# A fused attention and MLP block: regrouped heads, single-pass denominators, gate rows behind the first logit slot, and another way of starting

## Chip, cores and metric

The kernel runs on one core of one Trainium2 chip. The metric is the device time of one execution in microseconds (us). PE is the matrix engine, DVE the vector engine, ACT the scalar (activation) engine, POOL the GpSimd engine, SP the engine whose queue issues most of the DMAs. The kernel writes every engine's instructions in a fixed order; semaphores make one engine wait for another.

## What is computed

The input is x of 2048 tokens by 512 features in bf16. The output is `g * a + (1 - g) * b`, where `g = sigmoid(sum(x * gate_w))` is one number per token. The reference, cut to its core:

```
# branch a: 32 heads of 16, 4 segments of 512 tokens
q, k, v = x@wq, x@wk, x@wv              # split into heads and segments
for s in range(4):
    p     = softmax(qs @ ks.T * 0.25 + causal_mask)
    a_dot = p @ vs
    a_mem = (phi(qs) @ M) / (phi(qs) @ z + 1e-6)     # phi(t) = t+1 if t>0 else exp(t)
    o     = gb * a_mem + (1 - gb) * a_dot            # gb = sigmoid(beta), per head
    M, z  = M + phi(ks).T @ vs, z + sum(phi(ks))
a = concat(o) @ wo
# branch b
b = (gelu(x @ w_gate) * (x @ w_up)) @ w_down         # inner width 1792
```

## The kernel before, in words

**Layout.** x is kept transposed in `xT`, features on partitions (4 chunks of 128), tokens along the free axis. q and k of a segment are kept transposed too, in tiles of 128 partitions that hold 8 heads of 16; `c` counts these four groups of heads, `pr = c // 2` the pair they are stored in. A tile of 128 partitions has four strips of 32, `j = 0..3`, each with an even and an odd head; the kernel keeps a second copy of k, `kO`, with the even heads cleared, so that odd heads can be multiplied with strips of 32.

**Phases.** At the start (`first_k`, from L523) PE multiplies a cleared tile six times (L529), then turns the 512 tokens of segment 0 with 16 identity matmuls (L550) into four groups of PSUM banks, and DVE and ACT copy these into `xT` (helper at L314 and L316). Then k of segment 0 is projected (L565), then q and v, and all gate projections of branch b for all segments (L475, evacuated by ACT with GELU at L647). Ahead of the last segment's gate projections stand the gate rows (`gate_rows`, L601): `x * gate_w` summed, 16 column-tiled matmuls with weights that DVE makes in four copies (L662); DVE transposes them (L610), POOL spreads them with 32 small copies over partitions (L618, L619), and behind the first logits ACT takes two exps (L624, L625) and DVE finishes `omz` (L628, L629). `G2` (the exp) is read by all attention results, `omz` by the output.

Then comes attention: 4 segments of 20 logit slots. A slot is 512 columns of row-tiled logits for 4 strips (L735) into two pairs of PSUM banks, two exps on ACT (L757) and two causal selects on POOL (L766). After every five slots two groups `pv` (L785) multiply the probabilities with v, four heads side by side in four column strips; DVE transposes the result (L803), divides, adds the memory part and writes it over `xT` (L829). PE fills the time between slots with column-tiled matmuls, all recorded at L479 by the helper `dense`: up projections (evacuated and multiplied with the GELU on DVE, L657), q, k and v of the next segment, the memory's denominators (`zbd`) and numerators (`Mbd`), and the down and output projections.

**Order.** A planner (`Sched`) writes the order of every engine before the kernel is built: tasks carry costs, priorities, dependencies and rings of buffers, and it gives each PSUM group its banks out of eight. What is written outside it (memsets, masks, loads, in L392 to L438) stands ahead of all its tasks on each engine. `NUPS` says how many of the 56 up groups go into each segment, `SEED` shuffles priorities.

**What the change touches.** `RINGS` (L322), the setup at L384 to L438 with `bd`, a mask of 8 blocks that POOL makes with two selects (L433, L435), after the memset of `vz[0]` (L428) and `hot8` (L429, L430); `first_k`; `gate_rows` and its task `later`; `lhs_rhs` (L709), the dependencies in `logit_slot` (L737), the heads of `pv_group` (L783), `phi` (L842), `m_update` with `zbd` (L921), `mem_den` (L933) and `mem_num` (L965, whose product at L981 is on DVE), and the beta and wo loads (L405, L407).

Today's denominators for a segment are 4 groups of 4 column-tiled matmuls that accumulate into one bank:

```
for c in range(NCH):
    dense(t, zbd[:, c * P:(c + 1) * P], PQ[(s, c // 2)][:, c % 2, :], c == 0, c == NCH - 1)
```

Of the kernel before, what the change touches and what calls it, by code (L numbers as in the profile page):

```python
# [11 lines left out]
BF = dt.bfloat16  # L12
# [24 lines left out]
NWARM = 6  # L37
NUPS = (28, 10, 9, 9)
ATT = 5
SEED = 1  # L40
# [248 lines left out]
def kernel(  # L289
# [22 lines left out]
    def copy(e, dst, src):  # L312
        if e == "ACT":
            nc.scalar.activation(dst, src, AF.Copy)  # L314
        else:
# [6 lines left out]
    RINGS = {"qT": 3, "kT": 3, "kO": 3, "pT": 12, "E": 1, "Q1": 1, "pq": 3,  # L322
             "pkT": 1, "pk": 2, "T": 2, "r": 2, "N": 2, "rm": 1, "Tm": 1, "Nm": 3,
             "osb": 3, "tt": 1}
# [34 lines left out]
    beta8 = ctile("beta8", [8, NCH])  # L359
    bd = ctile("bd", [P, 8, DH])  # L360
    hot8 = ctile("hot8", [8, 8, DH])
# [3 lines left out]
    zbd = ctile("zbd", [P, NCH * (P + 2)])  # L365
# [5 lines left out]
    omg = ctile("omg", [P, NCH], F32)  # L371
    ebr = ctile("ebr", [P, NCH], F32)
    tb = ctile("tb", [P, NCH], F32)
# [13 lines left out]
    gwB = p1.tile([P, FC, 32], BF, name="gwB", tag="gwB")  # L387
# [3 lines left out]
    xn, ident, warm = wdn[:, 0:KT, :], wdn[:, KT, 0:P], wdn[:, KT + 1, :]  # L391
    nc.vector.memset(warm, 0.0)  # L392
# [12 lines left out]
    nc.sync.dma_start(beta8[:, :], A_beta.rearrange("(c h) -> h c", h=8))  # L405
    load_w(nc.sync, wup, B_w_up)
    load_w(nc.sync, wo, A_wo)  # L407

    def ext(at):
        return add("EXT", 0, lambda e: None, lat=at)  # L410

    a_xn = [ext(2700), ext(3200)]
    a_x = [None, ext(18000), ext(22000), ext(26000)]
    a_wk, a_wq = [ext(3900), ext(4200), ext(4500), ext(4800)], ext(5500)
# [12 lines left out]
    nc.vector.memset(zbd[:, :], 0.0)  # L427
# [8 lines left out]
                            compare_op=ALU.is_ge, fill=0.0, base=DH - 1, channel_multiplier=-1)  # L436
    nc.gpsimd.memset(vz[1][:, :, :], 1.0)
# [85 lines left out]
    def first_k():  # L523

        tl = {}

        def f_warm(_):
            for i in range(NWARM):
                nc.tensor.matmul(pair(w)[:, 0, :], lhsT=warm[:, 0:P], rhs=warm,  # L529
                                 start=True, stop=True)  # L530
        w = add("PE", 427 * NWARM, f_warm, prio=-2000, alloc=["pair"])
# [3 lines left out]
        def f_open(_):  # L535
            for i in range(2):
                for h in range(2):
                    tl["x", h, i] = pair(op, h)[:, i, :].rearrange("p (f m) -> p f m", f=2)
                tl["k", i] = pair(op, 2 + i)
                QK[("k", 0, i)] = rtile("kT", [P, 2, L])  # L540
# [4 lines left out]
        for h in range(2):  # L545
            for i in range(2):
                def f_t(_, h=h, i=i):
                    for f in range(2):
                        for m in range(2):
                            nc.tensor.matmul(tl["x", h, i][:, f, m * P:(m + 1) * P],  # L550
                                             lhsT=xn[:, 2 * h + m, (2 * i + f) * P:(2 * i + f + 1) * P],
                                             rhs=ident, start=True, stop=True)
                prev = add("PE", 430, f_t, prio=-1999, deps=[prev, a_xn[h]])
                dst = xT[:, 2 * i:2 * i + 2, h * L // 2:(h + 1) * L // 2]
                xe[h, i] = add("ACT" if i else "DVE", 600,
                               lambda e, dst=dst, k=(h, i): copy(e, dst, tl[("x",) + k][:, :, :]),
                               prio=0, deps=[prev], frees=[(("pair", h), op)])
        a_x[0] = xe[1, 1]
# [3 lines left out]
        for fc in range(FC):  # L562
            def fn(_, fc=fc):
                for c in range(NCH):
# [4 lines left out]
                       deps=[last, xe[0, fc // 2], xe[1, fc // 2], a_wk[fc]])  # L569
# [26 lines left out]
    def gate_rows(prio):  # L596
# [11 lines left out]
        def f_tt(e, t):  # L608
            tl["tt"] = rtile("tt", [P, QB, 32], F32, p1)
            nc.vector.transpose(tl["tt"][:, :, :].rearrange("p a b -> p (a b)"), t[:, :])  # L610

        def f_sp(e):
            z = tl["tt"]
            for s in range(NSEG):
                src = slice(32 * s, 32 * s + 32)
                for j in range(4):
# [4 lines left out]
                        z[src, :, :].rearrange("p (kt a) b -> p a kt b", a=4)[:, j, :, 0])  # L621

# [9 lines left out]
        tt = evac("DVE", g, box, f_tt, alloc=["tt"])  # L632
        TAB["zsp"] = add("POOL", 4000, f_sp, deps=[tt], prio=6, frees=[("tt", tt)])

        def later():
            TAB["g2"] = add("ACT", 500, f_ex, deps=[TAB["zsp"], TAB["first_x"]], prio=2)
            TAB["omz"] = add("DVE", 250, f_om, deps=[TAB["g2"]], prio=5)
        TAB["later"] = later
# [26 lines left out]
    def f_bps(t):  # L665
        nc.tensor.matmul(t[:, 0:NCH], lhsT=hot8[:, :, :].rearrange("p a b -> p (a b)"),  # L666
                         rhs=beta8[:, :], start=True, stop=True)
# [5 lines left out]
    def f_eb(e):  # L673
        nc.vector.reciprocal(ebr[:, :], omg[:, :])
# [4 lines left out]
    def f_wo(e):  # L679
        for c in range(NCH):  # L680
            nc.vector.tensor_scalar_mul(wo[:, c, :], wo[:, c, :], omg[:, c:c + 1])
# [6 lines left out]
    for s in range(NSEG):  # L688
        if s == 3:
            gate_rows(-960 + 20 * s)  # L690
        for hp in range(HS // 2):
            gate_pair(s, hp, -959 + 20 * s + hp)
            if s == 1 and hp == HS // 2 - 1:
                g, box = group("bps", 60, f_bps, -922, [a_be])
                t_tb = evac("ACT", g, box, lambda e, t: nc.scalar.activation(
                    tb[:, :], t[:, 0:NCH], AF.Tanh, scale=0.5), cost=250)
# [7 lines left out]
    opened = add("EXT", 0, reopen, deps=list(GM.values()) + [TAB["zsp"]])  # L704
# [3 lines left out]

    def lhs_rhs(s, c, e, j, kt, qb, nq):  # L709
        pr, i = c // 2, c % 2  # L710
# [5 lines left out]
    def logit_slot(s, t):  # L716
# [20 lines left out]
        deps = [EVQK[("q", s, c)]]  # L737
        if w <= 2:
            deps.append(EVQK[("k", s, c)])
        if w >= 2:  # L740
            deps.append(EVQK[("o", s, c)])
# [5 lines left out]
        if w == 4 and c % 2 == 1:  # L747
            pr = c // 2
            frees = [(n + "T" if n != "o" else "kO", first_ev[(n, s, pr)]) for n in "qko"]
            if s == 0:  # L750
# [354 lines left out]
```

## Time and profile before

| what | value |
|---|---|
| median of 3 runs | 274.99 us (274.38 to 275.15) |
| the profiled execution | 274.56 us, of which the span of its instructions is 272.7 us |
| busy in the span: PE, ACT, DVE, POOL | 266.6, 211.6, 171.5, 106.2 us |
| start of k's projection (L565) | 6.05 us |
| gate rows (L601) start | 52.97 us |
| first logit slot (L735) | 66.14 us |
| last slot of the last segment | 255.96 us |
| denominators (L479 on zbd) | 48 matmuls, 3.1 us busy |
| Nm product on DVE (L981) | 12 times 855 ns |

All starts are counted from the span's start. A row of a timeline gives start, length, engine, line, operation, the tiles it writes and reads, how many instructions were merged, and in brackets how long its engine was idle before and who ended that. Matmuls overlap in the array, so that one matmul's recorded length is longer than the distance between the starts of two.

### The profile page before, as it was taken

How to read it: one execution, taken by the hardware profiler on the slowest of the kernel's cores; microseconds unless marked ns; L12 is line 12 of the kernel's file. 1: busy time of each engine (PE TensorE's matmuls, PEld its weight loads, DVE VectorE, ACT ScalarE, POOL GpSimd, SP SyncE). 2: the span in 40 equal slices, each digit the busy share in tenths (PEclk: the TensorE clock that was granted, in tenths of full speed). 3: DMA queues.
4: the chain of work that ended last, by engine and by line, in shares of the span. 5: the costliest groups of instructions: out<-in, count | busy, mean ns of one | idle time of the engine just before them, and what ended most of it. 6: DMA issues, size and time to landing. Idle time of an engine off the chain costs nothing.

```text
span 272.7 us, 10273 instructions
## 1 busy us (share of the span) xinstructions
PE 266.6 (98%) x4569; PEld 127.0 (47%) x4575; DVE 171.5 (63%) x323; ACT 211.6 (78%) x234; POOL 106.2 (39%) x209
## 2 busy tenths in 40 slices
PE   7999999999999999999999999999999999999995
PEld 4444444444444554454444454444444444444454
DVE  3340003000888898989998989999858698765140
ACT  3445555646987799998978998899998999889812
POOL 8100000070343444355444545455555456664500
PEclk9999999999999999999999999999999999999999
DMA  7994790000023000220001121000000000000002
GB/s 210 369 135 97 256 352 10 0 0 2 5 45 38 2 2 2 41 43 2 2 23 22 42 41 41 5 2 2 22 22 4 22 24 2 22 22 22 22 5 78
DMA packets 22244, 14.02 MB, mean 51 GB/s; under 512 B 14136, under 2 KB 21176, under 8 KB 22200
## 3 DMA queue, kind: packets, MB, share of 16 engines
q1 hardware_dynamic: 21624, 12.85, 17.9%
q8 instruction: 35, 0.57, 0.9%
q10 hardware_dynamic: 576, 0.52, 0.6%
q14 instruction: 9, 0.07, 0.1%
HBM read 8.13 MB, written 2.10 MB: 37 GB/s over the span
## 4 chain that ended last, share of the span: by engine, by line
PE 97%; ACT 1%; issue 1%; DVE 0%; ACTq 0%
PE ps L479 57%; PE ps L475 20%; PE ps L735 10%; PE ps L785 6%; PE ps L565 1%; PE ps L529 1%; ACT pT L757 1%; PE ps L894 1%; PE ps L550 0%; PE ps L601 0%; DVE xT L316 0%; ACT osb L1017 0%; DVE wdn L392 0%; PE ps L666 0%; ACTq L1017 0%
## 5 line engine op out<-in xcount | busy, mean ns | idle before, releaser
L757 ACT ACTIVATE pT<-ps 128x1024 bf16<-128x1024 f32 x160 | 153.7, 1031 | 15.9 <-PE ps L735 14.7
L766 POOL TENSOR_SCALAR_AFFINE_SELECT pT<-pT 128x512 bf16<-128x512 bf16 (+1 forms) x160 | 94.3, 592 | 104.0 <-ACT pT L757 103.2
L479 PE MATMUL ps<-wdn,G 128*32 128x512 bf16 (+1 forms) x952 | 59.1, 368 | 0.2 <-ACT pT L757 0.2
L479 PE MATMUL ps<-xT,wup 128*32 128x512 bf16 x896 | 55.5, 380 | 0.0
L657 DVE TENSOR_TENSOR G<-ps,G 128x512 bf16<-128x512 f32 x56 | 37.8, 680 | 18.3 <-PE ps L479 18.0
L475 PE MATMUL ps<-xT,wga 128*128 128x512 bf16 x219 | 48.4, 379 | 0.4 <-issue 0.2
L647 ACT ACTIVATE G<-ps 128x1024 bf16<-128x1024 f32 x28 | 28.7, 1024 | 23.5 <-PE ps L475 22.8
L475 PEld LDWEIGHTS <-wga 128*128 128x128 bf16 x224 | 21.7, 98 | 26.4 <-issue 0.4
L803 DVE STREAM_TRANSPOSE T<-ps 128x512 f32<-128x512 f32 x32 | 22.7, 708 | 17.7 <-PE ps L785 11.6
L479 PEld LDWEIGHTS <-wup 128*32 128x32 bf16 x896 | 23.2, 96 | 21.1 <-issue 2.1
L479 PEld LDWEIGHTS <-G 128*32 128x32 bf16 x952 | 22.4, 96 | 19.4 <-issue 4.2
L618 POOL COPY G_87<-tt 32x16 f32<-32x16 f32 x16 | 3.1, 195 | 47.8 <-DVE tt L610 47.2
L735 PE MATMUL ps<-qT,kT 16*128 16x256 bf16 (+2 forms) x320 | 17.4, 274 | 0.0
L735 PE MATMUL ps<-qT,kO 32*128 32x128 bf16 (+2 forms) x320 | 17.3, 272 | 0.0
L479 PE MATMUL ps<-wo,xT 128*32 128x512 bf16 (+1 forms) x272 | 16.5, 367 | 0.0
L479 PEld LDWEIGHTS <-xT 128*32 128x32 bf16 x464 | 11.5, 96 | 10.3 <-issue 2.1
L735 PEld LDWEIGHTS <-kT 16*128 16x128 bf16 x320 | 6.8, 92 | 18.9 <-issue 18.8
L735 PEld LDWEIGHTS <-kO 32*128 32x128 bf16 x320 | 6.9, 92 | 12.1 <-issue 12.0
L479 PE MATMUL ps<-xT,wq 128*32 128x512 bf16 x192 | 12.5, 380 | 0.0
L479 PE MATMUL ps<-xT,wk 128*32 128x512 bf16 x192 | 12.5, 380 | 0.0
L1017 ACT ACTIVATE osb<-ps,omz 128x512 bf16<-128x512 f32 (+1 forms) x8 | 5.1, 635 | 9.4 <-PE ps L479 9.4
L479 PE MATMUL ps<-wv,xT 128*32 128x512 bf16 x192 | 12.4, 381 | 0.0
(116 smaller groups left out, 249.6 us busy)
## 6 DMA issues: line engine op xcount, KB each, us to landing
out_dram<-osb SPq DMA_DIRECT2D x15, 128.0 KB, 1.8
wup<-in_B_w_up_dram SPq DMA_DIRECT2D x1, 1792.0 KB, 8.2
wdn<-in_B_w_down_dram SPq DMA_DIRECT2D x1, 1792.0 KB, 13.7
wga<-in_B_w_gate_dram SPq DMA_DIRECT2D x1, 1280.0 KB, 10.2
wq<-in_A_wq_dram SPq DMA_DIRECT2D x1, 512.0 KB, 4.8
wga<-in_B_w_gate_dram SPq DMA_DIRECT2D x1, 512.0 KB
wv<-in_A_wv_dram SPq DMA_DIRECT2D x1, 512.0 KB, 7.3
wo<-in_A_wo_dram SPq DMA_DIRECT2D x1, 512.0 KB, 9.3
```

What stands on the lines that cost most here:

```text
L475: nc.tensor.matmul(t, lhsT=lhsT, rhs=rhs, start=start, stop=stop)
L479: nc.tensor.matmul(t[a, :], lhsT=lhsT[:, a], rhs=rhs, start=start, stop=stop, tile_position=(0, 32 * j), skip_group_check=True)
L529: nc.tensor.matmul(pair(w)[:, 0, :], lhsT=warm[:, 0:P], rhs=warm, start=True, stop=True)
L618: nc.gpsimd.tensor_copy(G2[dst, s, :], z[src, :, 0])
L647: ge = evac("ACT", g, box, lambda e, t: nc.scalar.activation(dst, t[:, :, :], AF.Gelu_apprx_tanh), cost=920, ring="pair")
L657: UPT[(s, hs)] = evac("DVE", g, box, lambda e, t: nc.vector.tensor_mul(G[:, s, hs, :], t[:, :], G[:, s, hs, :]))
L735: nc.tensor.matmul(A[j // 2][:, j % 2, at * P:(at + nq) * P], lhsT=l, rhs=r, start=True, stop=True, tile_position=(32 * j, 0))
L757: nc.scalar.activation(pT[(s, t, h)][:, :, :], A[h][:, :, :], AF.Exp, scale=0.25)
L766: nc.gpsimd.affine_select(out=v, in_=v, pattern=pat, compare_op=ALU.is_ge, fill=0.0, base=0, channel_multiplier=-1)
L785: nc.tensor.matmul(t[32 * j:32 * j + 32, qb * P:(qb + nq) * P], lhsT=vz[s % 2][:, kt, h * VW:h * VW + 32], rhs=pT[(s, t0 + w, j // 2)][:, ...
L803: nc.vector.transpose(TT[key][:, e, :, :].rearrange("p a b -> p (a b)"), t[:, :])
L1017: nc.scalar.activation(bx["o"][:, cols], bank(first)[:, cols], AF.Copy, scale=f)
```

## The change

The same work is grouped otherwise. Strip j of a logit slot takes its head from group (c + j) % 4 instead of c, so that the four column strips of a `pv` result hold heads of all four groups; strip q holds group q. `mem_num` follows, and `mem_den` becomes one pass of four column-tiled matmuls, each with another moving operand; its weights come from `zmask`, which 16 small copies on DVE make out of `bd` during setup. The rows of `wo` are loaded in the new order with 16 loads instead of one, and a second set of beta in the new order with 16 more. All q, k and kO of a segment are due at its first slot, with rings of 4 instead of 3. The gate rows move behind slot 0; their transposed tile uses the ring `Tm`, and the POOL copies become four tasks. The Nm product moves from DVE to POOL; `phi` writes in place. PE warms up with eleven matmuls of 256 columns on the constant 1.0 instead of six of 512 on a cleared tile; x of segment 0 is turned token tile by token tile, evacuated by DVE (0, 2), ACT (1) and both (3). `NUPS` and `SEED` change.

```diff
-NWARM = 6
-NUPS = (28, 10, 9, 9)
+NWARM = 11
+NUPS = (27, 9, 9, 11)
...
-SEED = 1
+SEED = 3
...
-    RINGS = {"qT": 3, "kT": 3, "kO": 3, "pT": 12, "E": 1, "Q1": 1, "pq": 3,
+    RINGS = {"qT": 4, "kT": 4, "kO": 4, "pT": 12, "E": 1, "pq": 2,
              "pkT": 1, "pk": 2, "T": 2, "r": 2, "N": 2, "rm": 1, "Tm": 1, "Nm": 3,
-             "osb": 3, "tt": 1}
+             "osb": 3}
...
+    zmask = ctile("zmask", [P, NCH, 8])
...
+    bsrc = A_beta.rearrange("(q j e) -> j e q", j=4, e=2)
+    nc.sync.dma_start(beta8[0:8, 0, :], A_beta.rearrange("(c h) -> h c", h=8))
+    for q in range(4):
+        for g in range(NCH):
+            nc.sync.dma_start(beta8[2 * q:2 * q + 2, 1, g:g + 1], bsrc[(q - g) % 4, :, q:q + 1])
     load_w(nc.sync, wup, B_w_up)
-    load_w(nc.sync, wo, A_wo)
+    for q in range(4):
+        for g in range(NCH):
+            r0 = P * q + 32 * ((q - g) % 4)
+            nc.sync.dma_start(wo[32 * q:32 * q + 32, g, :], A_wo[r0:r0 + 32, :])
...
-    nc.vector.memset(zbd[:, :], 0.0)
+    nc.vector.memset(zbd[:, :, :], 0.0)
+    nc.vector.memset(zmask[:, :, :], 0.0)
...
                             compare_op=ALU.is_ge, fill=0.0, base=DH - 1, channel_multiplier=-1)
+    for q in range(4):
+        for g in range(NCH):
+            j = (q - g) % 4
+            a = slice(32 * j, 32 * j + 32)
+            nc.vector.tensor_copy(zmask[a, q, 2 * g:2 * g + 2], bd[a, 2 * j:2 * j + 2, 0])
...
+        one = nc.const_aps.tensor(1.0, (P, 256), BF)
+
         def f_warm(_):
             for i in range(NWARM):
-                nc.tensor.matmul(pair(w)[:, 0, :], lhsT=warm[:, 0:P], rhs=warm,
+                nc.tensor.matmul(pair(w)[:, 0, 0:256], lhsT=one[:, 0:P], rhs=one,
                                  start=True, stop=True)
-        w = add("PE", 427 * NWARM, f_warm, prio=-2000, alloc=["pair"])
+        w = add("PE", 214 * NWARM, f_warm, prio=-2000, alloc=["pair"])
...
+        for kt in range(KT):
+            def f_t(_, kt=kt):
+                for f in range(FC):
+                    nc.tensor.matmul(tl["x", kt][:, f, :], lhsT=xn[:, kt, f * P:(f + 1) * P],
+                                     rhs=ident, start=True, stop=True)
+            prev = add("PE", 430, f_t, prio=-1999, deps=[prev, a_xn[kt]])
+            for i, e in ((0, "DVE"), (1, "ACT")):
+                if kt < 3 and i != kt % 2:
+                    continue
+                fs = slice(0, FC) if kt < 3 else slice(2 * i, 2 * i + 2)
+
+                def f_x(e, kt=kt, fs=fs):
+                    copy(e, xT[:, fs, kt * P:(kt + 1) * P], tl["x", kt][:, fs, :])
+                xe[kt, i] = add(e, 600 if kt < 3 else 350, f_x, prio=0, deps=[prev],
+                                frees=[(("pair", kt // 2), op)])
+        a_x[0] = add("EXT", 0, lambda _: None, deps=list(xe.values()))
...
-                       deps=[last, xe[0, fc // 2], xe[1, fc // 2], a_wk[fc]])
+                       deps=[last, xe[2, 0], xe[1, 1], xe[3, fc // 2], a_wk[fc]])
...
-        tt = evac("DVE", g, box, f_tt, alloc=["tt"])
-        TAB["zsp"] = add("POOL", 4000, f_sp, deps=[tt], prio=6, frees=[("tt", tt)])
-
-        def later():
-            TAB["g2"] = add("ACT", 500, f_ex, deps=[TAB["zsp"], TAB["first_x"]], prio=2)
-            TAB["omz"] = add("DVE", 250, f_om, deps=[TAB["g2"]], prio=5)
-        TAB["later"] = later
+        tt = evac("DVE", g, box, f_tt, deps=[opened], alloc=["Tm"])
+        sp = [add("POOL", 1000, f_sp(s), deps=[tt], prio=6, frees=[("Tm", tt)])
+              for s in range(NSEG)]
+        TAB["g2"] = add("ACT", 500, f_ex, deps=sp + [TAB["first_x"]], prio=2)
+        TAB["omz"] = add("DVE", 250, f_om, deps=[TAB["g2"]], prio=5)
...
-        pr, i = c // 2, c % 2
+        pr, i = divmod((c + j) % 4, 2)
...
-        deps = [EVQK[("q", s, c)]]
-        if w <= 2:
-            deps.append(EVQK[("k", s, c)])
-        if w >= 2:
-            deps.append(EVQK[("o", s, c)])
+        deps = [EVQK[(n, s, q)] for n in "qko" for q in range(NCH)] if t == 0 else []
...
-                for j in range(4):
-                    h = 8 * c + 2 * j + e
-                    nc.tensor.matmul(t[32 * j:32 * j + 32, qb * P:(qb + nq) * P],
+                for q in range(4):
+                    j = (q - c) % 4
+                    h = 8 * q + 2 * j + e
+                    nc.tensor.matmul(t[32 * q:32 * q + 32, qb * P:(qb + nq) * P],
                                      lhsT=vz[s % 2][:, kt, h * VW:h * VW + 32],
                                      rhs=pT[(s, t0 + w, j // 2)][:, j % 2, at * P:(at + nq) * P],
                                      start=(kt == 0), stop=(kt == KT - 1),
-                                     tile_position=(0, 32 * j), skip_group_check=True)
+                                     tile_position=(0, 32 * q), skip_group_check=True)
...
+            nc.vector.tensor_mul(zbd[:, :, 0:8], zmask[:, :, :],
+                                 Macc[:, :, 0, DH:DH + 1].to_broadcast((P, NCH, 8)))
...
-            for c in range(NCH):
-                dense(t, zbd[:, c * P:(c + 1) * P], PQ[(s, c // 2)][:, c % 2, :], c == 0,
-                      c == NCH - 1)
-        g, box = group("den", 4 * MM, mms, prio,
+            for q in range(4):
+                nc.tensor.matmul(t[32 * q:32 * q + 32, :], lhsT=zbd[:, q, :],
+                                 rhs=PQ[(s, q // 2)][:, q % 2, :], start=True, stop=True,
+                                 tile_position=(0, 32 * q), skip_group_check=True)
+        g, box = group("den", MM, mms, prio,
...
-            dense(t, Mbd[:, c, :, :].rearrange("p h d -> p (h d)"), PQ[(s, c // 2)][:, c % 2, :],
-                  True, True)
+            for q in range(4):
+                j = (q - c) % 4
+                nc.tensor.matmul(t[32 * q:32 * q + 32, :],
+                                 lhsT=Mbd[:, q, 2 * j:2 * j + 2, :].rearrange("p h d -> p (h d)"),
+                                 rhs=PQ[(s, q // 2)][:, q % 2, :], start=True, stop=True,
...
-            nc.vector.tensor_mul(NMt[(s, c)][:, :, :, :], bx["T"][:, :, :, :],
+            nc.gpsimd.tensor_mul(NMt[(s, c)][:, :, :, :], bx["T"][:, :, :, :],
...
-                        qk_group(s + 1, c, which, n1 + 5 * c - 8, AE)
+                        qk_group(s + 1, c, which, n1 - 10 + 1.5 * c, AE)
...
-                TAB["later"]()
+                gate_rows(-5)
```

## The prediction

> **What bounds the kernel now.** I read the page's engine shares first, then the chain that ended last, then the busy times over the four attention segments, then the timeline of the places that the change touches.
>
> ```profile
> PE 266.6 (98%) x4569; PEld 127.0 (47%) x4575; DVE 171.5 (63%) x323; ACT 211.6 (78%) x234; POOL 106.2 (39%) x209
> ...
> PE 97%; ACT 1%; issue 1%; DVE 0%; ACTq 0%
> ```
>
> PE is busy 98% of the span and is 97% of the chain, so what is added to or taken from PE's stream of work goes into the time at full price, and so does any hole made in it. The other engines cost nothing until PE waits for them.
>
> ```profile
> core 0: us, PE busy (x) PEld busy (x) DVE busy (x) ACT busy (x) POOL busy (x), PEclk, DMA share, GB/s
> 66.14:120.72 54.58, 54.58 (x1151) 26.29 (x1151) 46.03 (x86) 48.55 (x55) 22.29 (x39) 1.00 0.12 20
> 120.72:171.21 50.49, 50.49 (x1069) 23.90 (x1066) 45.89 (x85) 45.34 (x52) 24.62 (x42) 1.00 0.11 26
> 171.21:214.64 43.43, 43.43 (x901) 20.16 (x898) 36.80 (x68) 40.15 (x44) 22.83 (x40) 1.00 0.04 12
> 214.64:255.96 41.32, 40.58 (x824) 18.77 (x821) 28.33 (x48) 37.49 (x41) 22.85 (x39) 1.00 0.06 19
> ```
>
> Each row is one segment, from its first logit slot to the next segment's (the last to its own last slot). PE fills all four, but ACT is at 86 to 92% and DVE at 68 to 91%: a late instruction on either reaches PE soon. Laying out the fillers between slots at 0.216 us per four column tiles of 512 gives 151.9 us; 79 slots take 0.44 us each beside them (a slot with 2.59 of fillers lasted 3.04), together 186.6 of the 189.8 measured. So about 3.2 us is M updates and stalls, and no better order can give back more.
>
> **The start, part by part.** These rows are the first 10 us.
>
> ```profile
> 1.26 2.74 PE L529 MATMUL ps<-wdn 128*128 128x512 bf16 x6 [1.26 <-DVE wdn L392]
> ...
> 3.79 1.69 PE L550 MATMUL ps<-wdn 128*128 128x128 bf16 x16
> 4.47 1.53 DVE L316 CAST xT<-ps 128x512 bf16<-128x512 f32 x2 [2.05 <-PE ps L550]
> 5.02 0.34 POOL L435 TENSOR_SCALAR_AFFINE_SELECT bd<-bd 128x128 bf16<-128x128 bf16 x1
> 6.00 3.16 PEld L565 LDWEIGHTS <-wk 128*128 128x128 bf16 x16 [0.69 <-DMA wk<-in_A_wk_dram]
> 6.05 3.61 PE L565 MATMUL ps<-xT,wk 128*128 128x512 bf16 x16 [0.56 <-DVE xT L316]
> ...
> 29.05 0.44 DVE L662 COPY gwB<-gw 128x32 bf16<-128x32 bf16 x4 [11.75 <-DMA gw<-in_gate_w_dram]
> ```
>
> The first k projection (L565) starts at 6.05, when the evacuations of x are done; its weight load waited for wk until 6.00. So the warm-up on a constant and the finer turning cannot start it before about 6.0: their price is 0, and at most 0.05 is to be had, because wk's landing covers them.
>
> What stands in the way is new. The diff builds zmask with 16 DVE copies of 32x2 out of bd, and in the built order they stand ahead of all evacuations of x on DVE, the first one waiting for POOL's last select on bd. POOL's list up to there is unchanged, so bd is done at 5.02 + 0.34 = 5.36. DVE takes its instructions in order: x waits behind it, though its transposes are ready by about 5.2. No row shows a 32x2 copy. Below, 16 copies at nothing; above, 16 x 0.178, the full duration of one gwB copy, 2.85. I take the distance between the starts of the four gwB copies, (0.44 - 0.178)/3 = 0.087, as the nearest row: 16 x 0.087 = 1.39. Then come three evacuations on DVE (token tiles 0 and 2, half of tile 3): k evacuations, two in 1.29 at 0.69 each, follow each other at 0.60, so 0.60 + 0.60 + 0.42 (between a 128x68 copy at 0.22 and 0.69), and 0.05 to PE. 5.39 + 1.39 + 1.62 + 0.05 = 8.45: PE starts **2.4 later** (1.0 to 3.9 by the bounds). From there to 66.14 PE has no hole above 0.2, so nothing swallows it. Setting bd's selects ahead of vz's memset would take most of it away.
>
> [...]
>
> In that time PE has nothing to do from about 5.2 to 8.45, 3.2 us. The rows show two speeds: the warm-up's six matmuls of 512 start 0.427 apart (2.74 less one duration of 0.63, over 5), L565's sixteen 0.215 apart; the granted clock reads 1.00 in both. PE had worked 3.9 us when the transposes grew faster, near 5.15. If it falls back to the slow pace, some 3.9 us are done at half speed again: up to 2.0 lost. Below, nothing: PE stood idle 0.56 before L565 and stayed fast. I take 0 and keep 2.0 as a case.
>
> [...]
>
> **Denominators.** Today each segment's den takes 16 column-tiled matmuls per group of four c, 48 in all (L479 on zbd, 3.1 us busy, starting 0.054 apart); now 4 per segment. 36 fewer x 0.054 = **-1.94** on PE. That four tiles with four different moving operands still run side by side is shown by L785: 20 matmuls in 0.55 to 0.66, where a quarter of their columns alone is 0.53. The rotation of heads over (c + j) % 4 changes no count and no shape of logits, PV or num.
>
> **Gate rows.** Today they stand between gate projections.
>
> ```profile
> 52.44 0.59 PE L475 MATMUL ps<-xT,wga 128*128 128x512 bf16 x2
> 52.97 1.05 PE L601 MATMUL ps<-xT,gwB 128*32 128x512 bf16 x16
> 54.17 0.59 PE L475 MATMUL ps<-xT,wga 128*128 128x512 bf16 x2 [0.16 <-issue]
> ```
>
> ```profile
> 54.95 0.19 POOL L618 COPY G_87<-tt 32x16 f32<-32x16 f32 x1 [47.22 <-DVE tt L610]
> 55.09 0.18 POOL L619 COPY omz<-tt 32x4 f32<-32x4 f32 x1
> 55.31 0.19 POOL L618 COPY G_87<-tt 32x16 f32<-32x16 f32 x1
> ```
>
> From the last L475 before (52.66) to the next (54.17) pass 1.51; 0.216 belongs to that L475, so the sixteen cost 1.30. Among column-tiled fillers they cost 0.87: **-0.43**. But their POOL copies, 32 in pairs of 0.365 (5.8 us), lost their cover. They ran under gate work; now, behind slot 0 (66.14 in this trace's time), they stand ahead of what the slots need. The sixteen end about 67.5, the DVE transpose (1.19 after their start, 0.72 long) at 68.4, 16 copies at 71.4, two selects of slot 0 (0.41 each) at 72.2, 16 copies at 75.1. On ACT the two exps of the gate (0.25 together) stand ahead of slot 2's exps and wait for that: slot 2's first exp runs 75.4 to 76.4 instead of from about 73.8. In the built order slot 3's logits write the bank that this exp frees. PE, through with slot 2 (73.4) and two up groups, would be there at 75.5: it waits 0.95. Behind it, the next k group needs a bank that DVE frees; on DVE the two omz operations wait for ACT's exps (75.5) ahead of a pkT minimum and that product, which ends at 77.35: another 0.55. A third wait, 0.2, is the second up group's, for the transpose's bank. Sum 1.7, less 0.2 lost in this stretch today (slot 0 lasted 4.01 for 3.45 + 0.44): **+1.5**. Below 0, if exps and fillers close up; above 3, if the copies stretch to one and a half times beside a busy DVE, which no row shows.
>
> **The rest, at nothing.** The Nm product goes from DVE (12 x 0.855 = 10.3) to POOL. POOL's price isn't shown; between its 128x512 select at 0.71 and the 2240-element memset at 1.97, I take 1.0. POOL is at 41 to 55% in the segments and covers it; its queue holds selects behind Nm, and PV waits for those: a late rm could cost some tenths per segment. DVE's relief can give back a part of the 3.2 us of losses. All projections of a segment are now due at its slot 0, with a ring of 4 for that. SP gets 16 small beta loads and 15 more for wo: at 0.45 to 0.5 an issue wup goes out 7 us later, at 34.5, wo and wdn by 43; wup is first read at 66.5, and wo's scaling, 43.25 today, has until the last gate projection. Beta is read near 41 plus the delay and lands near 38. Fillers of the four segments change from 44.8, 41.3, 33.8, 32.0 (before the last slot) to 45.2, 38.9, 34.5, 32.2, and 13.1 behind the last slot stay: PE's balance is kept. I take 0 for all this, within 1.0 either way.
>
> **Sum.** +2.4 - 1.94 - 0.43 + 1.5 = **+1.5** on the profiled execution, 274.56 (span 272.7 and 1.86 around it): 276.1. The median of the runs shown, 274.99, lies 0.43 above it, so **276.5**.
>
> **Rivals.**
> - *PE falls to half pace behind the hole at the start.* For: the hole of 3.2 us, and 3.9 us of work needed at first. Against: the 0.56 of idle that did nothing. +2.0: 278.5.
> - *The gate chain is hidden.* If POOL's copies end by 73.5, ACT never waits, and 1.5 goes: 275.0, no change. For: the planner has 8 banks, and PE has up groups to do. Against: 5.8 us of copies, and slot 3 on the bank of slot 2's exp.
> - *Faster: the fuller DVE queue is what makes today's losses.* DVE loses 10.3 us in segments 1 to 3, 0.909 busy in segment 1. If that takes 1.5 to 2 of the 3.2 us, and the gate chain costs less than 0.5, den and gate rows outweigh the start: 274.99 + 2.4 - 2.4 - 1.8 = 273.2. It decides from 0.8 net gained. Against: PE was busy 50.49 of that segment's 50.49.
> - *The constant warm-up and token tiles start k sooner, as written.* Only if x isn't behind zmask on DVE; wk's landing at 6.00 caps it.
>
> **How the numbers follow.** About 0.3%, 0.8 us, is what a measurement can tell from no change. The worked case has 0.42 (275.4 to 277.6 by its own terms), half pace 0.23, the hidden chain 0.20, faster 0.15. All of the first two end slower, the third within 0.3%. The range takes the first three and their bounds: 274.2 to 278.8.
>
> **What would show it.** Right: DVE's first x evacuation starts near 6.8, behind 16 copies; L584 starts near 8.4; den has 12 matmuls; ACT waits for POOL near 1.5 us ahead of its two short exps. Wrong: copies far from 0.087, L584 below 7.5, L584's sixteen at 0.43 apart (half pace), no ACT wait for POOL, or segments 1 to 3 shorter by more than the den's 0.65 each and their fillers.

## The result, and the profile after

The changed kernel takes 284.0 us (median of 4 runs, 282.27 to 284.73), where the kernel before took 274.94 (274.38 to 275.15) beside it: 1.032 times as long, 95% interval 1.027 to 1.037. The forecast was 276.5, and its range ended at 278.8. The profiled execution of the changed kernel is the longest of its four, 284.73; its span is 283.0, 10.3 longer than that of before.

From the page of the changed kernel, the shares of PE and the other engines, PE's granted clock over 40 slices (the part of the full clock that PE was given, in tenths), and the chain's shares by engine:

```profile
PE 268.6 (95%) x4539; PEld 127.9 (45%) x4544; DVE 169.9 (60%) x328; ACT 212.0 (75%) x235; POOL 116.3 (41%) x221
...
PEclk9579999999997999999999999999999999999999
...
PE 85%; DVE 6%; POOL 4%; ACT 3%; issue 1%; POOLq 0%; ACTq 0%; DVEq 0%
```

PE is still the engine with the most work, but it stands idle for 14.4 us of the span, where it was 6.1: 8.3 of the 10.3 are holes in PE's stream, and its busy time is 2.0 longer. Of the chain 15% now lies elsewhere, where it was 3%: 6% DVE, 4% POOL, 3% ACT. The clock row shows something that before had nowhere: a fall in slices 2 and 3 and another in slice 13. The four segments of the changed kernel, from first slot to first slot:

```profile
core 0: us, PE busy (x) PEld busy (x) DVE busy (x) ACT busy (x) POOL busy (x), PEclk, DMA share, GB/s
73.36:132.47 59.11, 56.55 (x1157) 27.53 (x1158) 48.77 (x92) 48.76 (x55) 29.27 (x72) 0.97 0.10 21
132.47:180.90 48.43, 48.34 (x1024) 22.78 (x1021) 40.64 (x73) 44.40 (x50) 28.31 (x46) 1.00 0.09 22
180.90:224.86 43.96, 43.96 (x913) 20.55 (x911) 35.62 (x65) 41.02 (x46) 24.38 (x43) 1.00 0.06 18
224.86:266.34 41.48, 40.94 (x829) 18.60 (x826) 26.84 (x46) 38.04 (x41) 25.94 (x43) 1.00 0.05 16
```

The first slot comes 7.22 later (73.36 for 66.14). The first segment is 4.53 longer, the second 2.06 shorter, the last two 0.53 and 0.16 longer, the tail 0.09 shorter: together the 10.3. The fillers laid between the slots changed by +0.43, -2.37, +0.65 and +0.21, so the last three segments only follow their share of work. What is lost is lost in two places, ahead of the first slot and in the first segment.

**Ahead of the first slot.** The timeline of the changed kernel around the start (start, length, engine, line, tiles, count, idle time before and who ended it):

```profile
5.04 0.34 POOL L445 TENSOR_SCALAR_AFFINE_SELECT bd<-bd 128x128 bf16<-128x128 bf16 x1
...
5.32 1.96 POOL L452 MEMSET vz_83<- 128x2240 bf16 x1
...
5.41 4.68 DVE L451 COPY zmask<-bd 32x2 bf16<-32x2 bf16 x16 [3.18 <-POOL bd L445]
...
7.22 0.52 POOL L453 MEMSET Mbd<- 128x512 bf16 x1
...
10.01 1.60 DVE L316 CAST xT<-ps 128x512 bf16<-128x512 f32 x3
...
11.67 2.72 PE L584 MATMUL ps<-xT,wk 128*128 128x512 bf16 x6 [6.90 <-DVE xT L316]
```

The shape of the delay is the predicted one: bd, 16 copies, three evacuations, then k. Its size is not: the copies take 4.68, PE stands idle for 6.90, and k starts at 11.67 instead of 6.05. The durations of the 16 copies (shortest, median, longest, in ns):

```profile
L451 DVE COPY zmask<-bd x16: 154/161/2353, 5.4 to 9.9; 32x2 bf16<-32x2 bf16 x16
```

One of them, the first, took 2353 ns; it ended at 7.77, just behind POOL's two memsets (the second ends at 7.74), in whose time it lay. The others last 0.16 each. Then the clock. The busy times of the changed kernel in five stretches (the number before the DMA share is the granted clock):

```profile
7.30:11.60 4.30, 0.00 (x0) 0.00 (x0) 4.14 (x19) 0.00 (x0) 0.45 (x1) 0.50 1.04 370
11.67:17.40 5.73, 5.73 (x14) 2.02 (x14) 0.00 (x0) 0.00 (x0) 0.00 (x0) 0.50 1.03 253
17.60:23.30 5.70, 5.65 (x27) 2.60 (x27) 3.03 (x7) 4.40 (x7) 0.00 (x0) 1.00 0.50 107
82.36:85.77 3.41, 1.47 (x28) 0.75 (x24) 2.70 (x5) 3.35 (x6) 3.00 (x6) 1.00 0.07 15
85.77:89.18 3.41, 3.41 (x49) 1.83 (x42) 1.79 (x4) 1.61 (x2) 0.81 (x2) 0.50 0.41 72
```

PE's hole begins at 4.77; the clock falls 2.5 later, and the half clock holds from 7.26 to 17.50. In it 14 matmuls of k start in 5.73, 0.427 apart; from 17.5 they are 0.216 apart. The 5.62 of a later start, 2.9 of half pace, less the 1.30 of gate rows that moved away, make the 7.22.

**In the first segment.** The gate rows behind slot 0, same kernel:

```profile
75.56 0.19 POOL L637 COPY G_89<-Tm 32x16 f32<-32x16 f32 x1 [67.81 <-DVE Tm L629]
...
82.42 0.26 ACT L644 ACTIVATE G_89<-G_89 128x64 f32<-128x64 f32 x1 [1.92 <-POOL G_89 L637]
...
82.81 0.44 DVE L648 TENSOR_SCALAR omz<-omz 128x16 f32<-128x16 f32 x1 [1.08 <-ACT omz L645]
...
83.74 0.40 PE L753 MATMUL ps<-qT,kO 32*128 32x512 bf16 x4 [1.07 <-ACT pT L770]
...
85.01 1.21 PE L494 MATMUL ps<-xT,wk 128*32 128x512 bf16 x16 [0.87 <-DVE G L675]
```

This is the predicted chain: POOL's copies until 82.5, ACT's short exps behind them (1.92 of idle), slot 3's logits behind the exp that frees their bank (1.07), the next k group behind DVE (0.87). Slots 0 to 3 lasted 4.04, 3.04, 3.31 and 6.2, where their fillers and the usual 0.44 make 4.0, 3.04, 2.17 and 3.57. The waits account for 2.1 (1.14 in slot 2, 0.95 in slot 3, by the traces of kernels below in which the clock stayed up and slot 3 lasted 4.52). The other 1.7 is the second fall of the clock, 85.77 to 89.18, behind a stretch in which PE was idle for 1.94 of 3.41.

### The profile page after: what moved, and what is told of

It reads as the page before. It is cut to its first block, busy times and chain, and to the rows that moved or that the text cites. A ratio compares the mean times of both kernels' runs of the same rounds, so it can differ in the third digit from the quotient of the medians.

```text
span 283.0 us, 10243 instructions
## 1 busy us (share of the span) xinstructions
PE 268.6 (95%) x4539; PEld 127.9 (45%) x4544; DVE 169.9 (60%) x328; ACT 212.0 (75%) x235; POOL 116.3 (41%) x221
## 4 chain that ended last, share of the span: by engine, by line
PE 85%; DVE 6%; POOL 4%; ACT 3%; issue 1%; POOLq 0%; ACTq 0%; DVEq 0%
PE ps L494 47%; PE ps L490 19%; PE ps L753 8%; PE ps L799 6%; ACT pT L770 2%; PE ps L584 2%; DVE zmask L451 2%; POOL G_89 L637 1%; POOL omz L638 1%; PE ps L978 1%; POOL vz_82 L438 1%; PE ps L906 1%; DVE xT L316 1%; DVE T L817 0%; DVE G L675 0%
## 5 line engine op out<-in xcount | busy, mean ns | idle before, releaser
L779 POOL TENSOR_SCALAR_AFFINE_SELECT pT<-pT 128x512 bf16<-128x512 bf16 (+1 forms) x160 | 91.6, 577 | 82.5 <-ACT pT L770 81.7
L494 PE MATMUL ps<-wdn,G 128*32 128x512 bf16 (+1 forms) x952 | 59.8, 368 | 0.0
L637 POOL COPY G_89<-Tm 32x16 f32<-32x16 f32 x16 | 3.4, 213 | 68.4 <-DVE Tm L629 67.8
L494 PEld LDWEIGHTS <-xT 128*32 128x32 bf16 x464 | 12.1, 96 | 9.8 <-issue 0.6
L629 DVE STREAM_TRANSPOSE Tm<-ps 128x512 f32<-128x512 f32 x1 | 0.7, 716 | 22.0 <-PE ps L620 22.0
L994 POOL TENSOR_TENSOR Nm<-Tm,rm 128x512 bf16<-128x512 f32 x12 | 13.3, 1109 | 1.2 <-DVE N L840 0.9
L314 ACT ACTIVATE kT<-ps 128x512 bf16<-128x512 f32 x7 | 4.0, 601 | 12.7 <-PE ps L584 12.2
L494 PE MATMUL ps<-xT,wq 128*32 128x512 bf16 x192 | 13.5, 401 | 0.0
```

The costliest lines, as they stand in the source:

```text
L494: nc.tensor.matmul(t[a, :], lhsT=lhsT[:, a], rhs=rhs, start=start, stop=stop, tile_position=(0, 32 * j), skip_group_check=True)
L637: nc.gpsimd.tensor_copy(G2[dst, s, :], z[src, :, 0])
L779: nc.gpsimd.affine_select(out=v, in_=v, pattern=pat, compare_op=ALU.is_ge, fill=0.0, base=0, channel_multiplier=-1)
L994: nc.gpsimd.tensor_mul(NMt[(s, c)][:, :, :, :], bx["T"][:, :, :, :], RMt[s][:, :, 2 * c:2 * c + 2][:, :, :, None] .to_broadcast((P, QB, 2, ...
```

## The experiments

The theory after reading the two traces, in two parts. **M:** the mask copies, held by POOL's memset and standing ahead of x on DVE, open PE's hole, and the hole brings the half clock; together some 9 us. **G:** the gate chain on POOL, ACT and DVE costs 2 to 4 in the first segment. The rivals: **S**, that the new warm-up and the turning by token tile make the late start; and, against G, that the first segment is longer through its new order.

**The mask copies out of the way.** They become a task of DVE's, behind gwB's copies near 30 us; all else stays.

```diff
-    for q in range(4):
-        for g in range(NCH):
-            ...
-            nc.vector.tensor_copy(zmask[a, q, 2 * g:2 * g + 2], bd[a, 2 * j:2 * j + 2, 0])
+    add("DVE", 2400, f_zm, deps=[a_gw], prio=4)
```

> The 16 zmask copies are issued later on DVE, behind the gwB copies near 30 us, where DVE is idle; nothing else moves. Theory M (the mask copies ahead of x's evacuations make the loss at the start): the first k projection starts near 6.0 instead of 11.67, its sixteen matmuls stand 0.216 apart, and the time falls by 5.6 + 2.9 = 8.5, from 284.0 to about 275.5. Theory S (turning x by token tile, or warming up on a constant, makes the loss): the time stays within 1 of 284.

275.31 us (274.44 to 278.6, 10 runs), 1.003 times before (0.9997 to 1.006). Its start:

```profile
5.33 1.97 POOL L447 MEMSET vz<- 128x2240 bf16 x1
...
5.91 0.42 DVE L316 CAST xT<-ps 128x256 bf16<-128x256 f32 x1 [0.38 <-ACT xT L314]
...
6.39 2.96 PE L579 MATMUL ps<-xT,wk 128*128 128x512 bf16 x13 [0.93 <-DVE xT L316]
```

POOL's memset is where it was, and the last evacuation of x runs beside it at 0.42: it isn't held. k starts at 6.39 and at full pace. 8.7 of the 9.1 us are gone, by the medians: the copies ahead of x make the loss at the start, hole and half clock together. The same profile, of a run of 276.94, still shows the gate chain (ACT idle 1.95 before its short exp; slots of 4.04, 3.04, 3.35 and 6.12, the last one at half clock from 76.79 on).

**The old start with the copies in place.** Warm-up on a cleared tile with six matmuls, turning by halves, as before the change.

```diff
-NWARM = 11
+NWARM = 6
...
+                    for f in range(2):
+                        for m in range(2):
```

> Warm-up on the cleared tile, turning and evacuation of x as before the change; the mask copies stay where the change put them. Theory M: DVE still reaches x only near 10.0, needs two evacuations instead of three, and k starts near 11.4 at half pace: 283 to 284. Theory S: k starts near 6.05 again and the time is about 275.5.

282.93 us (281.34 to 284.47, 4 runs), 1.031 (1.025 to 1.036):

```profile
10.02 1.27 DVE L316 CAST xT<-ps 128x512 bf16<-128x512 f32 x2
11.34 5.04 PE L581 MATMUL ps<-xT,wk 128*128 128x512 bf16 x16 [6.38 <-DVE xT L316]
```

The evacuations still start at 10.02, k at 11.34. S is rejected: the way PE warms up and x is turned moves k by 0.33, one evacuation less, and not by 5.6.

**POOL's memsets out of the way.** vz[1] and Mbd are cleared by DVE behind gwB, the copies stay ahead of x.

```diff
-    nc.gpsimd.memset(vz[1][:, :, :], 1.0)
-    nc.gpsimd.memset(Mbd[:, :, :, :], 0.0)
+    add("DVE", 2500, f_ms, deps=[a_gw], prio=4)
```

> The memsets of vz[1] and Mbd leave POOL and are issued on DVE behind gwB near 30 us; the mask copies stay. Theory M with its first part (the first mask copy, 2.35 long, is held by POOL's memset that runs beside it): the first copy takes 0.17 like the others, x's evacuations start near 7.8, k near 9.5, so 2.2 less from the shorter wait, and up to 2.9 more if the clock then stays up: 279 to 282. Rival (the first copy is slow for another reason, such as the wait for bd): its 2.35 stay and the time is 284.

280.91 us (279.43 to 282.77, 4 runs), 1.022 (1.016 to 1.027). The copies in its profile:

```profile
L451 DVE COPY zmask<-bd x16: 156/160/168, 5.4 to 7.8; 32x2 bf16<-32x2 bf16 x16
```

No long one is left; x is evacuated from 7.83 instead of 10.01, k starts at 9.48, and the half clock still comes (8.67 to 15.49). So POOL's memsets held the first copy for 2.2, and without that the sixteen copies still make a hole of 4.17, which is large enough.

**The same copies in another order.** By strip of partitions: four copies on one strip, then four on the next.

```diff
-    for q in range(4):
-        for g in range(NCH):
-            j = (q - g) % 4
+    for j in range(4):
+        for q in range(4):
+            g = (q - j) % 4
```

> The 16 mask copies stay at the start, but are written strip by strip, so that four in a row work on the same 32 partitions. If a copy can follow closely only on one of the same strip (0.077 against 0.176 in the changed kernel's trace), the copies behind the first take 12 x 0.077 + 3 x 0.176 = 1.45 instead of 2.23 and x's evacuations start 0.8 earlier, near 9.2. Rival (the distances go with the place in the mask, not with the strip): 10.0 again.

281.11 us in one run:

```profile
5.42 3.54 DVE L451 COPY zmask<-bd 32x2 bf16<-32x2 bf16 x16 [3.18 <-POOL bd L445]
9.00 1.62 DVE L316 CAST xT<-ps 128x512 bf16<-128x512 f32 x3
```

The first four copies, of one strip, are all held: they end together at 7.77 to 7.80 (2353 to 2161 ns). From there the starts are about 0.07 apart on one strip and 0.167 at each change of strip. x is evacuated from 9.00, 1.0 sooner, k starts at 10.67. In the changed kernel nearly every copy changes the strip. That is why sixteen of them cost 0.155 each, and not gwB's 0.087: gwB's four lie on the same partitions.

**PE kept busy in the hole.** If half pace comes from the hole, idle work on PE must prevent it: 32 matmuls of 256 columns on the constant between the turning and k.

```diff
+        def f_fill(_):
+            for i in range(32):
+                nc.tensor.matmul(tl["k", 0][:, 0, 0:256], lhsT=one[:, 0:P], rhs=one,
+                                 start=True, stop=True)
+        last = add("PE", 214 * 32, f_fill, prio=-1999, deps=[prev])
```

> The mask copies stay; PE does 32 more matmuls of 256 columns on the constant between turning x and the first k projection, up to 3.5 to 7 us of work into a bank that is written anew afterwards. Theory M with its second part (the idle PE falls to half pace and pays 2.9 for it): k still starts near 11.7 but at 0.216 apart if the filling is long enough, about 281. Rival (the half pace comes from something else than the idle time): k's matmuls stay 0.427 apart and the time is 284.

283.18 us (282.2 to 284.85, 4 runs), 1.030 (1.026 to 1.035). The filling matmuls were too few: they ended at 8.95, and 2.73 of hole was left, most of the stretch 8.62 to 12.03. That stretch and the next:

```profile
8.62:12.03 3.41, 0.68 (x4) 0.33 (x4) 2.91 (x13) 0.00 (x0) 0.00 (x0) 1.00 1.04 364
12.04:15.45 3.41, 3.31 (x9) 1.18 (x8) 0.00 (x0) 0.00 (x0) 0.00 (x0) 0.50 1.32 256
```

The clock stayed up through the first and fell behind it, at 12.04. k had begun at 11.68, so that nearly all of the half pace that followed fell on k, its matmuls again 0.427 apart; but it lasted 3.4 us, not 10. With 64 of them:

> As e4_pe_filled with 64 instead of 32 filling matmuls (6.9 at full pace, so they reach to about 12.0). If idle PE is what halves the clock: no drop before the gate projections, k starts near 12.0 at 0.216 apart, and the time is 284.0 - 2.9 + 0.3 = 281.4, of which up to 1.6 hangs on the half clock in the first slots. Rival: k's matmuls 0.427 apart again, 284.

289.75 us (288.28 to 291.27, 4 runs), 1.056 (1.053 to 1.059). PE in its profile:

```profile
5.36 7.54 PE L582 MATMUL ps<-const-bfloat16-1.0 128*128 128x256 bf16 x64
12.73 3.61 PE L588 MATMUL ps<-xT,wk 128*128 128x512 bf16 x16
```

Sixteen matmuls of k in 3.61: full pace, as expected. The time is spoilt by something else. The filling matmuls' planned cost of 214 ns each moved the planner's whole order: gwB's copies, which wait for a late load, went ahead of v's evacuations on DVE, and PE stood idle for 5.17 near 25 us. So 62 filling matmuls that the planner takes to cost nothing:

> As e7_pe_filled_64, with 62 filling matmuls that the planner counts as nothing, so that the order of all other work is the changed kernel's. Idle PE halves the clock: k starts near 11.7 to 12.2, its matmuls 0.216 apart, no drop of the clock before the first slots: 284.0 - 2.9 = 281.1, 1.6 less where the first slots keep the clock too. Rival: 0.427 apart, 284.

282.2 us (281.74 to 282.77, 4 runs), 1.026 (1.023 to 1.028):

```profile
5.90 8.34 PE L582 MATMUL ps<-const-bfloat16-1.0 128*128 128x256 bf16 x62
14.07 2.10 PE L588 MATMUL ps<-xT,wk 128*128 128x512 bf16 x8
```

k follows, behind one gap of 0.43, at 0.215 apart, and its clock never falls. But the clock rose only at 8.46 here, so that the first filling matmuls ran at half pace, and k began 2.4 later than the 11.67 at which x lets it. The first slot comes at 72.9, little before the 73.36; most of the 1.8 below 284.0 is the first segment, where the clock stayed up (57.60 for 59.11). The three kernels show that the hole brings half pace. None turned k's full pace into time: the filling matmuls stand where the hole was, or end behind it.

**The gate rows back in their old place,** on top of the first edit, with their copies planned at 1450 each.

```diff
-                gate_rows(-5)
+                TAB["later"]()
...
+        if s == 3:
+            gate_rows(-960 + 20 * s)
```

> The mask copies late as in e1_mask_late, and the gate rows, their POOL copies and their two exps back where they stood before the change (ahead of the last segment's gate projections). Theory G (what is left of the loss is POOL's 5.8 of copies under the first slots, with ACT, DVE and PE waiting behind them, and the half clock that this idle time brings in some runs): slots 2 and 3 lose their 2.1 of waiting, the gate rows cost 0.43 more on PE, no half clock: about 273. Rival R (the first segment suffers from the regrouped heads, whose q, k and kO are all due at slot 0): the time stays near 275.3.

275.91 us (275.58 to 277.55, 7 runs), 1.006 (1.004 to 1.009). The waits went as G expects: slots 2 and 3 last 3.04 and 1.85, and the clock stays up. The time did not follow, and by the time alone the rival R stood. The planner made another order, and the time went elsewhere: the last segment took 41.6 for 31.1 of fillers and 8.4 of slots, 2.1 of loss, where before lost 0.9 there, and the first still lost 2.2, where before lost 1.1. A kernel that changes the whole order can't price one chain.

**Only the plan of the gate rows corrected.** On top of the first edit, POOL's four tasks are planned at 1460 each, which is what they last (four pairs of 0.365), instead of 1000. Their place and number stay.

```diff
-        sp = [add("POOL", 1000, f_sp(s), deps=[tt], prio=6, frees=[("Tm", tt)])
+        sp = [add("POOL", 1460, f_sp(s), deps=[tt], prio=6, frees=[("Tm", tt)])
```

> The mask copies late as in e1_mask_late; gate rows stay behind slot 0, but each of the four POOL copy tasks is planned at 1460 ns, as measured, instead of 1000, so that the planner puts the gate's exps behind slot 3's on ACT. Theory G: ACT waits for POOL no more, slots 2 and 3 last 3.0 and 2.7 for their fillers, no half clock, and 275.3 falls to about 272.3, den's 1.94 and the gate rows' 0.43 below the kernel before. Rival (POOL's copies are the loss wherever the exps stand, because they delay the selects): 274 or more.

274.99 us (272.89 to 275.54, 12 runs), 0.998 (0.995 to 1.000). ACT in its first segment:

```profile
75.80 1.95 ACT L773 ACTIVATE pT<-ps 128x1024 bf16<-128x1024 f32 x2
77.61 0.29 ACT L639 ACTIVATE G<-G 128x64 f32<-128x64 f32 x1
77.76 0.24 ACT L640 ACTIVATE omz<-omz 128x16 f32<-128x16 f32 x1
```

The short exps now stand one slot later, behind exps that have their input, and wait for nothing. Slots 2 and 3 last 3.03 and 2.71, the clock stays up, and the profiled span is 271.4 for the 275.1 of the first edit, of which some 1.6 was that run's half clock in slot 3. By its profile G is confirmed, and R is answered: the regrouped heads are still here, and beyond its fillers and 0.44 for each slot the first segment loses 0.7, before 1.1. The planner moved work here too (1.7 of fillers from the first segment into the third and fourth), and the second and third segments lose 0.5 and 0.7 more than in the first edit's kernel, so that the whole gain is less than the chain's. The medians, 275.31 and 274.99, hardly tell the two kernels apart. The runs fall into two groups, 272.9 to 273.6 and 275.0 to 275.5, so the same kernel was run again:

> e6_spread_cost once more, since its runs lay in two groups, 272.9 to 273.6 and 275.0 to 275.5. If the two groups come from PE's clock at the start (it rises one window of 3.4 later), both groups are there again and a profile of a slow run shows k's first matmuls 0.427 apart. Rival (something of that one chip): one group only, near 273.

273.3 us (272.82 to 275.54, 12 runs), 0.996 (0.994 to 0.998): 8 runs at 272.8 to 273.6, 4 at 274.8 to 275.5. Both groups are there again, on another chip. Its segments, in the columns of the first such table:

```profile
64.78:117.64 52.86, 52.85 (x1093) 25.05 (x1092) 44.40 (x84) 49.47 (x57) 27.70 (x71) 1.00 0.13 23
117.64:166.52 48.88, 48.64 (x1024) 22.55 (x1021) 41.26 (x77) 44.96 (x52) 29.50 (x45) 1.00 0.09 25
166.52:212.81 46.29, 45.70 (x973) 21.66 (x970) 34.74 (x65) 42.43 (x47) 24.96 (x43) 1.00 0.04 14
212.81:254.42 41.61, 41.33 (x833) 18.74 (x830) 27.40 (x47) 37.91 (x41) 25.59 (x43) 1.00 0.05 16
```

The first slot is at 64.78, 1.36 ahead of before: the gate rows' 1.30, and hardly more. PE's stream has no hole left in the first segment.

**PE busy through the start of that kernel.** Thirteen warm-up matmuls and ten filling matmuls ahead of k, which the planner takes to cost what it did.

```diff
-NWARM = 11
+NWARM = 13
...
+        last = add("PE", 1, f_fill, prio=-1999, deps=[prev])
```

> e6_spread_cost with 13 instead of 11 warm-up matmuls and 10 more on the constant between turning x and the first k projection, planned at no cost, so that PE has no hole before k. If the upper group comes from holes in PE's first 6 us, which let the clock rise late or fall again, only the group near 273 is left. Rival: both groups stay, or all runs pay 0.3 to 1.0 for the added matmuls.

273.51 us (273.07 to 274.01, 6 runs), 0.995 (0.993 to 0.996): only one group, and the lowest interval of the study, half a percent below the kernel before. The price that the rival names is there too: the first slot comes at 65.54 for 64.78, and the median lies 0.3 above that of the lower group's 13 runs in the two series of runs without them (273.18). That the upper group comes from short holes in PE's first 6 us fits this; no profile caught a run of that group, so it stays an inference.

**The denominators made four times as dear.** Each of the four matmuls is done four times in that kernel, which gives the same sums and the old count, 16 per pass.

```diff
-            for q in range(4):
+            for q in list(range(4)) * 4:
```

> e6_spread_cost with each segment's four denominator matmuls done four times over (the result is the same), in the same order otherwise: as many matmuls as before the change. Theory (PE's stream is the bound, so the 36 matmuls are worth their 0.054 each): 1.94 more in segments 1 to 3, about 276.0 beside e10. Rival (a part is hidden in waits of the segments): 1 or less.

275.34 us (274.22 to 277.21, 12 runs), 1.003 (1.000 to 1.005). Its runs lie in two groups as well, six and six, and a median between two groups prices nothing; group beside group, this kernel is some 1.6 above the same kernel without the added matmuls. The three segments that hold a den (the first three) grow by 0.62, 0.47 and 0.30, 1.39 in all. So the 36 matmuls are worth 1.4 to 1.6 of the predicted 1.94; about 0.5 of it lies in waits.

## Why the prediction was wrong, step by step

- **The mask copies: the step that failed.** The prediction saw the place (16 copies in order ahead of x, behind bd) and took their price from gwB's copies, 16 x 0.087 = 1.39, with 2.85 as the upper end. They cost 4.6: x started at 10.01 for the expected 6.8. Some 2.3 of that 3.2 is the first copy, held by POOL's memsets; the other 1.0 is fifteen copies at 0.155 instead of 0.087. The row was the nearest in size, but it differed in two things that the built order showed: gwB's copies lie on one set of partitions with POOL idle, while these change the strip each time, and POOL's memsets stand right behind bd's select, beside the copies. The three evacuations and the 0.05 to PE came as expected (11.67 less 10.01, 1.66 for 1.67).
- **Half pace: taken at nothing, the second failure.** With the hole at 6.9 instead of 3.2, the case with chance 0.23 came true. It cost 2.9 at the start, not 2.0, since the clock rose only at 17.50. The 0.56 of idle that argued against it was no evidence on a hole of several us. It can come at the predicted size too: in the changed kernel the clock fell 2.5 into the hole, and in the kernel with 32 filling matmuls the hole was 2.73, and the clock fell behind it. (The 1.00 that the prediction read as granted to the warm-up was no reading: the clock's record begins with its first rise, at 5.12 in that trace.)
- **Where the hole went.** "From there to 66.14 PE has no hole above 0.2, so nothing swallows it" held: the 7.22 is 5.62 + 2.9 - 1.30.
- **Gate rows' place, -0.43:** right. Ahead of the first slot 1.30 is gone, and behind it 0.88 pass from their first matmul (73.68) to the next up projection (74.56).
- **The gate chain, +1.5:** right in every link, POOL to ACT to slot 3's bank, DVE to the k group. The waits are 2.1 for 1.7. Of POOL's 32 copies, which the upper bound stretched to one and a half times, 31 took 0.18 to 0.20, as before the change, and one 0.47, beside a DVE instruction that started with it (78.12). Left out was what such a hole does to the clock, another 1.7 in the profiled run.
- **Denominators, -1.94:** right within about 0.5, 1.4 to 1.6.
- **The rest at nothing:** right. Nm on POOL takes 12 x 1.08 for the 1.0 assumed, the last three segments follow their fillers. What Nm's move does by itself wasn't tried.
- **The rivals.** Half pace came, on top of a start twice as late. The hidden chain didn't. The fuller DVE queue wasn't what cost before: segments 1 to 3 shrank by 1.37, their fillers by 1.51. The constant warm-up brought nothing of its own: with x free of the copies, k starts at 6.39 and 5.96, for 6.05.

The mask copies' 3.2, the half clock's 2.9 at the start and 1.7 in slot 3, and 0.4 of longer waits in the gate chain make 8.2, which with the predicted +1.5 is 9.7 of the 10.3.

The runs show both halves of the first failure, and not what is behind them. The first copy took 2353 ns beside POOL's memset, and with the memsets late the longest of the sixteen took 168; it also lasted through the next memset, and no trace shows by what it was held. In the changed kernel the copies behind the first start 0.167 to 0.182 apart at a change of strip and 0.076 to 0.080 without; what makes a change dearer isn't shown.

On the clock the prediction looked at one long hole. In the changed kernel it also fell, at 85.77, behind a stretch of 3.41 with 1.94 idle in two pieces, of 1.07 and 0.87: there gaps that added up did it.

## What to carry to other kernels

A small instruction is priced by a row that agrees with it in partitions and in what runs beside it, not only in size (here 2353 ns for 156 to 168 beside POOL's memset, and 0.167 to 0.182 apart for 0.076 to 0.080 at a change of strip): look at what the other engines have in their queues at that time. The hole in PE had two prices here, 5.62 of later start and 2.9 of half clock behind it; add up PE's idle time over some 3.4 us, not gap by gap, since 1.94 in two pieces was enough. And a planner that believes a wrong duration places a waiting instruction ahead of ready ones: correcting one cost, 1000 to 1460, took 3.7 off the profiled span, some 1.6 of it half clock. In time, 13 of the corrected kernel's 24 runs took 272.8 to 273.6, and the first edit's runs whose clock stayed up 274.4 to 275.5; the other 11 lie at 274.8 to 275.5, and why is open.

## What the runs showed of the hardware that was not expected

- A DVE copy of 32x2 took 2353 ns when it started 0.09 behind a POOL memset of 1.96, and outlasted that memset and the next (to 7.77; the memsets ended at 7.28 and 7.74). With POOL's memsets late all sixteen took 156 to 168. An evacuation of x from PSUM beside the same memset took 0.42.
- Copies of 32x2 on the same 32 partitions start 0.07 to 0.08 apart, on changing ones 0.17 to 0.18 (changed kernel and strip order).
- In the traces all changes of the granted clock within one execution are multiples of 3.413 us apart (7.26, 17.50, 85.77 and 89.18 in the changed kernel); where the first lies differs between executions (3.85 in the changed kernel, 5.12 before the change, 8.46 with 62 filling matmuls). It fell behind stretches with 1.94 (changed kernel), 1.99 (memsets late) and 1.87 (mask copies late) of idle, and not behind 1.82 and 1.90 (32 and 64 filling matmuls). It rose behind stretches with as much as 0.50 of idle (old start: k began at 11.34, and the clock came back at 14.26), and not behind 0.81 (memsets late) and 0.99 (changed kernel: k began at 11.67, and the clock came back at 17.50). The idle times are read from modelled ends, so that the borders are rough.
- In the kernel with late mask copies, runs with a mean clock of 1.0 took 274.4 to 275.5, at 0.993 and 0.994 276.7 to 276.9, at 0.988 278.5: nearly 2 us for each stretch at half clock. A mean clock ranks runs only where the start is the same, since the record begins with the first rise and a slow start isn't in it: with 62 filling matmuls the mean is 1.0, though they ran at half pace until 8.46, and with the old start two runs at 0.994 took 284.3 and 284.5, two at 0.988 281.3 and 281.5.
